# Two neighbouring blocks in one transfer, two products of one weight in one matmul, and a new order of work

## The chip, the cores and the metric

The kernel runs on one core of a Trainium2 chip. Its time is the device time of one execution in microseconds. The core's engines run beside each other and are tied by semaphores: TensorE (PE, with PEld for its weight loads), VectorE (DVE), ScalarE (ACT), GpSimd (POOL), and SyncE (SP), which here only issues transfers (DMAs). 16 DMA engines move the bytes between the chip's main memory and the on-chip SBUF. PE writes its products to PSUM, which has eight banks of 512 fp32 columns.

## What is computed

An attention over the channels (normalised along N) is followed by a soft mixture of experts, all in fp32, with B = 4, N = 5056, C = 256, 8 experts of 4 slots each:

```python
qn = q / (norm(q, axis=1) + 1e-06);  kn = k / (norm(k, axis=1) + 1e-06)
a = softmax(kn.transpose(0, 2, 1) @ qn / tau)          # [B, C, C]
x = (v @ a).reshape(B * N, C)
logits = x @ phi                                       # [B*N, 32]
slot_input = softmax(logits, axis=0).T @ x             # 32 slots, 4 to an expert
slot_out = relu(slot_input @ w1[e]) @ w2[e]            # for each expert e
out = softmax(logits, axis=1) @ slot_out               # [B*N, C]
```

## The kernel before

Everything large is moved in blocks of 1 MiB: 128 partitions with a row of 8 KB each. There are 40 blocks of q and k together (`raw0` to `raw39`, ten to a batch), 20 of v, 10 of v transposed on the host (`x4` to `x13`; for the other v blocks PE transposes, L492), 8 of w1, 8 of w2, and 20 MiB of output. In main memory each 8 KB row of an input is followed by 512 bytes of padding; the output has none. SBUF holds 23 slots of one block. The table `SLOTS` gives each block its slot, and a block may be loaded when the last reader of the slot's former block is done. Since all transfers are issued by SP, one after another, a load that waits for its slot holds up every load behind it. At most eight transfers are under way: each has one of eight semaphores and waits for that one's former transfer.

What happens to one q/k block `u` (four tiles of 128 rows): `square` (ACT, L301 and L303) writes the squares, `add` (DVE, L321) sums them for the column norms. A part of the tiles (`NS[u]`, two to four of four from `u` = 1 on, 117 tiles in all) is split into a rounded high part and a low rest: `cast` (ACT, L288) writes the high part, `low` (POOL, L292) subtracts it. `score` (L345) then multiplies on PE: for a split tile and each half `m` of the key's columns three products of 256 columns (high key with high query, high key with low query, low key with high query), for a tile that is not split one product in plain fp32. All of them add into the same 256 columns of `S`, and the two halves `m` lie in one PSUM bank. At the end of a batch `att_evict` (ACT, L368) copies `S` to SBUF, and `att_cols` to `att_m` (L373 to L457) make the softmax and from it the matrix `M` that turns v into logits.

For a v block: `logits` (PE, L507 and L512), copies and maxima (ACT L535, DVE L539, L545), and, in groups of three and two blocks, exponents and `gather` (PE, L612). After the last group come the experts: `up` (PE, L762, needs w1), `down` (PE, L795, needs w2), and then the output: `out_mul` (PE, L830 and L845), `out_evict` (ACT and DVE in turn, L862) and `store` (SP, L866 to L872). The weights w2 come in two halves, `w2_0_*` for output columns 0 to 127 and `w2_1_*` for the rest; outputs named `oh` need only one half. The last loads are those of `w2_1_*`.

The order of all of it is written out: the steps are put in a list `plan`, and the table `ORDER` says in which order they are recorded. `BANKS` gives each PSUM tile its bank. `wake` (L255) multiplies ones with ones: eight such products stand ahead of the first score.

Of the kernel before, what the change touches and what calls it, by code (L numbers as in the profile page):

```python
# [8 lines left out]
F32 = mybir.dt.float32  # L9
# [15 lines left out]
NT = [3 if u % (2 * UB) == 2 * UB - 1 else 4 for u in range(NU)]  # L25
# [4 lines left out]

SAME = set()
# [6 lines left out]
WAKES = ((-8, 8),)  # L38


ORDER = [
# [60 lines left out]
]  # L102
SLOTS = {
# [64 lines left out]
}  # L168


def run(plan):
    for x in ORDER:
# [927 lines left out]
```

## Time and profile before

| | us |
|---|---|
| time, median of 3 runs | 271.57 (271.47 to 271.7) |
| span of the profiled execution | 269.6 |
| what lies around the span, against the median | 2.0 |
| PE, POOL, ACT, DVE busy in the span | 244.9, 169.6, 207.1, 201.0 |
| transfers of SP's queue, as a share of 16 engines' span | 98.8% |

How to read it: the busy times say how much each engine had to do, not which of them sets the end. For that one looks at what runs without a gap, at what the last work waited for, and at how far ahead of its use each transfer was issued. The profiled execution's own time beside its span was not recorded; the 2.0 us are the difference to the median.

### The profile page before, as it was taken

Reading aid. Unit: us, or ns where it says so; the run is one execution under the profiler, and the core shown is the slowest. Engines: PE = TensorE matmul, PEld = TensorE weight load, DVE = VectorE, ACT = ScalarE, POOL = GpSimd, SP = SyncE. Lnnn points to the kernel's source line nnn. Section 1 sums busy time; section 2 is a strip of 40 time slices with the busy share of each in tenths; the row PEclk is TensorE's granted clock in tenths of the full one; section 3 lists DMA queues with packets and bytes.
Section 4 is the critical chain, followed back from the end, with each engine's and each line's share of the span. In section 5 each row is a group of like instructions: output and inputs, shape, how many; then the busy total and the mean of one; then the engine's idle time right before and its main releaser. Section 6 shows DMA issues by size and latency. Waiting matters only on the chain.

```text
span 269.6 us, 6368 instructions
## 1 busy us (share of the span) xinstructions
PE 244.9 (91%) x2490; PEld 205.4 (76%) x2490; DVE 201.0 (75%) x406; ACT 207.1 (77%) x331; POOL 169.6 (63%) x135
## 2 busy tenths in 40 slices
PE   6999999999999999999999999999999889989300
PEld 6799899999998987879879968985647677666200
DVE  1388688978799989889998788897785747795400
ACT  3999899999999999999999987586826536566200
POOL 1399989999999998989999999731206030000000
PEclk9999999999999999999999999999999999999555
DMA  7999999999999999999999999999999999999995
GB/s 272 428 424 419 417 419 420 423 418 416 424 414 419 422 417 422 423 414 416 421 421 418 420 427 413 420 420 422 413 423 422 412 418 395 420 424 422 424 425 227
DMA packets 15725, 110.80 MB, mean 411 GB/s; under 512 B 1872, under 2 KB 1872, under 8 KB 3024
## 3 DMA queue, kind: packets, MB, share of 16 engines
q1 hardware_dynamic: 15696, 110.40, 98.8%
q8 instruction: 19, 0.31, 0.5%
q14 instruction: 10, 0.08, 0.1%
HBM read 89.43 MB, written 20.97 MB: 409 GB/s over the span
## 4 chain that ended last, share of the span: by engine, by line
PE 78%; DMA 11%; DVE 2%; ACT 1%; issue 1%; SPq 0%; ACTq 0%
PE S L345 42%; PE L L512 7%; PE G L612 7%; PE T L492 6%; DMA w<-in_moe_w_dram 6%; PE op_None L845 4%; DMA out_dram<-o 3%; PE op L830 3%; DMA raw<-in_qk_dram 3%; PE H L762 2%; PE O L795 1%; PE Mp L445 1%; ACT o L862 1%; PE S L354 1%; PE nn L373 1%; PE aTp L433 1%
## 5 line engine op out<-in xcount | busy, mean ns | idle before, releaser
L292 POOL TENSOR_TENSOR hl<-raw,hl 128x512 fp32r<-128x512 f32 x117 | 146.5, 1291 | 14.3 <-ACT hl L288 14.3
L321 DVE TENSOR_TENSOR A<-sq,A 128x512 f32<-128x512 f32 (+1 forms) x144 | 94.5, 690 | 20.6 <-ACT sq L303 18.5
L345 PE MATMUL S<-hl 128*128 128x256 f32 x702 | 100.0, 292 | 0.0
L345 PEld LDWEIGHTS S<-hl 128*128 128x128 f32 x702 | 89.1, 190 | 3.5 <-issue 2.3
L303 ACT ACTIVATE sq<-raw 128x2048 f32<-128x2048 f32 (+2 forms) x40 | 71.6, 1806 | 0.2 <-DMA raw<-in_qk_dram 0.2
L288 ACT CAST hl<-raw 128x1024 fp32r<-128x1024 f32 (+1 forms) x69 | 61.0, 916 | 2.9 <-DMA raw<-in_qk_dram 1.4
L345 PE MATMUL S<-raw 128*128 128x256 f32 x156 | 38.3, 381 | 1.7 <-DMA raw<-in_qk_dram 1.7
L345 PEld LDWEIGHTS S<-raw 128*128 128x128 f32 x156 | 27.7, 190 | 5.2 <-DMA raw<-in_qk_dram 2.5
L492 PE MATMUL T<-ident,v 128*128 128x128 f32 x156 | 21.8, 274 | 0.5 <-DVE maxs L539 0.5
L710 POOL TENSOR_TENSOR nat<-nat,cm 128x1280 f32<-128x1280 f32 x4 | 9.4, 2352 | 19.0 <-DVE cm L707 19.0
L725 POOL TENSOR_TENSOR nat<-nat,cs 128x1280 f32<-128x1280 f32 x4 | 9.4, 2348 | 16.9 <-DVE cs L722 16.9
L862 ACT COPY o<-op_None 128x512 f32<-128x512 f32 x22 | 12.0, 592 | 10.2 <-PE op_None L845 9.0
L512 PE MATMUL L<-x,M 128*32 128x256 f32 (+1 forms) x320 | 19.3, 379 | 0.0
L492 PEld LDWEIGHTS T<-ident,v 128*128 128x128 f32 x156 | 17.8, 141 | 1.8 <-DVE maxs L539 0.7
L612 PE MATMUL G<-v,dn 128*32 128x256 f32 x312 | 18.7, 380 | 0.0
L830 PE MATMUL op<-cT,so 32*128 32x256 f32 x144 | 17.5, 417 | 0.7 <-ACT so L817 0.4
L862 DVE COPY oh<-op 128x256 f32<-128x256 f32 x36 | 12.9, 411 | 5.3 <-PE op L830 5.0
L862 DVE COPY o<-op_None 128x512 f32<-128x512 f32 x22 | 13.9, 680 | 2.7 <-PE op_None L845 2.6
L830 PEld LDWEIGHTS op<-cT,so 32*128 32x128 f32 x144 | 12.3, 183 | 4.3 <-ACT o L862 1.5
L612 PEld LDWEIGHTS G<-v,dn 128*32 128x32 f32 x312 | 10.7, 110 | 6.3 <-issue 0.5
L512 PEld LDWEIGHTS L<-x,M 128*32 128x32 f32 x320 | 10.3, 110 | 5.7 <-issue 0.7
L862 ACT COPY oh<-op 128x256 f32<-128x256 f32 x36 | 11.9, 384 | 2.7 <-PE op L830 2.7
(122 smaller groups left out, 279.8 us busy)
## 6 DMA issues: line engine op xcount, KB each, us to landing
raw<-in_qk_dram SPq DMA_DIRECT2D x38, 1024.0 KB, 13.6
v<-in_v_dram SPq DMA_DIRECT2D x16, 1024.0 KB, 13.8
w<-in_moe_w_dram SPq DMA_DIRECT2D x16, 1024.0 KB, 19.8
out_dram<-o SPq DMA_DIRECT2D x11, 1024.0 KB, 10.2
x<-in_vt_dram SPq DMA_DIRECT2D x10, 1024.0 KB, 13.5
out_dram<-oh SPq DMA_DIRECT2D x8, 1024.0 KB, 8.8
v<-in_v_dram SPq DMA_DIRECT2D x4, 896.0 KB, 13.8
raw<-in_qk_dram SPq DMA_DIRECT2D x2, 768.0 KB, 11.5
```

The source lines that it names most:

```text
L288: act.copy(parts(u, lo, hi)[:, :, 0::2, :], raws[u][:, lo:hi])
L292: pool.tensor_tensor(hl[:, :, 1::2, :], raws[u][:, lo:hi], hl[:, :, 0::2, :].bitcast(F32), op=ALU.subtract)
L303: act.activation(sqs[u][:, n : NT[u]], raws[u][:, n : NT[u]], AF.Square)
L321: dve.tensor_tensor(a[r], s[r, j], a[r], op=ALU.add)
L345: pe.matmul(S_[:, m], l, r, start=first, stop=False, skip_group_check=True)
L492: pe.transpose(tp[:, P * jj : P * jj + P], vtile(p, 4 * h + jj)[:, P * m : P * m + P], ident)
L512: pe.matmul(L[S * g : S * g + S, :n, :], M[:, m, :], x[:, :n, S * g : S * g + S], start=m == 0 and g not in void, stop=m == 1, skip_group_ ...
L612: pe.matmul(gp[S * g : S * g + S, :C], dn[:, x, j, :], vtile(p, j), start=x == 0 and j < G, stop=x == n - 1 and j >= G,)
L710: pool.tensor_tensor(nat[b], nat[b], st[b]["cm"].broadcast_to([P, 8 * PB, S]), op=ALU.subtract)
L830: pe.matmul(ops[b, p, hf, g], so[r, hf], cT[b][r, 8 * p : 8 * p + 8, :].rearrange("s j t -> s (j t)"), start=True, stop=True,)
L845: pe.matmul(ops[b, p, hf, g][:, h, :], cT[b][r, 4 * i : 4 * i + 4, :].rearrange("s j t -> s (j t)"), rhs[r], start=True, stop=True,)
L862: (dve.tensor_copy if g % 2 else act.copy)(dst, ops[b, p, hf, g])
```

## The change

- **Transfers.** The 86 input blocks are put by the host into two arrays in main memory, `one` (rows of 8 KB) and `two` (two blocks side by side, rows of 16 KB; both with the same 512 bytes behind each row). The list `GROUPS` names 8 blocks that come alone and 39 pairs. A pair needs two neighbouring slots that are free at the same time, and both blocks land together. The list `OUTS` does the same for the output: 17 stores, four of them pairs of 2 MiB. The output array now has rows of 16 KB, without padding; blocks that are stored alone fill half of such a row. All bytes are the same.
- **Slots.** 9 slots are tiles as before (numbers 0 to 8), 14 are neighbours in one tile, `arena`. `SLOTS` is new.
- **Score.** The two products that have the high key as weight become one of 512 columns; the two halves of the columns are added later. So `S` takes two banks a batch, one for each `m`. `att_evict` adds the halves, on DVE instead of ACT.
- **Wake.** Ten products of ones ahead of the first score instead of eight; one more that stood near the end moves to the start too, and one of three goes to the stretch of the stores.
- **Order.** `ORDER`, `SLOTS` and `BANKS` are new throughout.

```diff
-WAKES = ((-8, 8),)
+WAKES = ((-8, 10),)
+NT_SLOTS, NA_SLOTS = 9, 14
+GROUPS = [
+    ("q0",), ("q1",), ("q2",), ("q3",), ("v4",), ("v9",), ("v14",), ("v19",), ("w1_4", "w1_5"),
...
+    arena = const.tile([P, NA_SLOTS, W], F32, name="arena")
...
+    def load(g):
+        n = sum(cols(x) for x in GROUPS[g])
+        src = (one, two)[len(GROUPS[g]) - 1][PLACE[g]]
+        sp.dma_start(run_of(GROUPS[g])[:, :n], src[:, :n])
...
     def score(u, j):
...
-                parts_ = [(hl[:, w, cols], hl[:, y, :]) for w, y in ((2, 0), (2, 1), (3, 0))]
-            for l, r in parts_:
-                pe.matmul(S_[:, m], l, r, start=first, stop=False, skip_group_check=True)
...
+            mul(m, hl[:, 2, cols], hl[:, 0:2, :].rearrange("p y c -> p (y c)"), 0, 2 * C)
+            mul(m, hl[:, 3, cols], hl[:, 0, :], 0, C)
...
     def att_evict(b, m):
-        act.copy(st[b]["ssb"][:, m], st[b]["S"][:, m])
+        both = st[b]["S"][m].rearrange("p (y c) -> p c y", y=2)
+        dve.tensor_reduce(mine(b, "ssb", [P, 2, C], "ssb")[:, m], both, axis=AX.X, op=ALU.add)
...
+    def store(g):
+        n = W // 2 if OUTS[g][0] in HALF else W * len(OUTS[g])
+        k, x = OPLACE[g]
+        sp.dma_start(oa[k][:, x * W : x * W + n], run_of(OUTS[g])[:, :n])
```

What stands on the queues now, in three places. **SP in the middle of the loads.** `raw` are q/k blocks, `x` transposed v blocks; `PE_49`, `DVE_49` and the like are the engines that a load waits for, `DMAHW` the transfers. Before:

```order
L266 DMA raw_946<-in_qk_dram 128x2048 [waits PE_49,DMAHW4_49,Activation_49,Pool_49]
L266 DMA raw_978<-in_qk_dram 128x2048 [waits DMAHW5_49,Activation_49]
L266 DMA raw_996<-in_qk_dram 128x2048 [waits DMAHW6_49,Pool_49]
L266 DMA raw_1014<-in_qk_dram 128x2048 [waits DMAHW7_49,PE_49]
L487 DMA x_1017<-in_vt_dram 128x2048 [waits DMAHW0_49,DVE_49]
L266 DMA raw_1082<-in_qk_dram 128x2048 [waits DMAHW1_49,PE_49,Pool_49]
```

And in the change, where these are the pairs `x4,x5`, `q32,q33`, `x6,x7`, `q30,q31`, then `v4` alone, then `x8,x9` and `v5,v6`:

```order
L260 DMA arena<-in_two_dram 128x4096 [waits DMAHW0_49,DMAHW5_49,Activation_49,Pool_49]
L260 DMA arena<-in_two_dram 128x4096 [waits DMAHW6_49,PE_49]
L260 DMA arena<-in_two_dram 128x4096 [waits DMAHW3_49,PE_49,DMAHW7_49,Activation_49,Pool_49]
L260 DMA arena<-in_two_dram 128x4096 [waits DVE_49,PE_49,DMAHW2_49,Activation_49,Pool_49]
L260 DMA arena<-in_one_dram 128x1792 [waits DMAHW5_49,DMAHW1_49,PE_49]
L260 DMA arena<-in_two_dram 128x4096 [waits Activation_49,Pool_49]
L260 DMA arena<-in_two_dram 128x4096 [waits PE_49,DMAHW4_49,Activation_49,Pool_49]
```

A load of the change waits for the readers of two former blocks, and carries twice the bytes.

**SP at the end, the stores.** Names: `oh` and `o` are output blocks. Before:

```order
L869 DMA out_dram<-oh_1_1_3125 128x2048
L866 DMA out_dram<-o_3_3184 128x2048
L866 DMA out_dram<-o_2_3221 128x2048
L866 DMA out_dram<-o_4_3241 128x2048
L866 DMA out_dram<-o_0_3218 128x2048
```

In the change:

```order
L260 DMA arena<-in_two_dram 128x4096 x13
L903 DMA out_dram<-arena 128x1024
L903 DMA out_dram<-arena 128x2048 x5
L903 DMA out_dram<-arena 128x4096
L903 DMA out_dram<-arena 128x2048
L903 DMA out_dram<-arena 128x4096
```

The last thirteen loads are all pairs; of the stores only four are, and a store of half a block now comes first.

**PE, the first blocks.** `hl` is a split pair of tiles, `raw` (`q` in the change) a block that is used as it came. Before:

```order
L345 MATMUL S_139<-raw_144 128x256 x4
L345 MATMUL S_139<-raw_131 128x256 x4
L345 MATMUL S_139<-hl_146 128x256 x6
L345 MATMUL S_139<-raw_163 128x256 x4
L345 MATMUL S_139<-hl_146 128x256 x6
```

In the change:

```order
L400 MATMUL S_0_138<-q_144 128x256
L400 MATMUL S_1_139<-q_144 128x256
L400 MATMUL S_0_138<-hl_160 128x512
L400 MATMUL S_0_138<-hl_160 128x256
L400 MATMUL S_1_139<-hl_160 128x512
L400 MATMUL S_1_139<-hl_160 128x256
```

Six products of 256 columns for a split tile became two of 512 and two of 256.

## Rows read from the trace of the kernel before

**Rows 1.** The page: span, and in 40 slices the DMA engines' busy tenths.

```profile
span 269.6 us, 6368 instructions
DMA  7999999999999999999999999999999999999995
GB/s 272 428 424 419 417 419 420 423 418 416 424 414 419 422 417 422 423 414 416 421 421 418 420 427 413 420 420 422 413 423 422 412 418 395 420 424 422 424 425 227
```

**Rows 2.** The page, part 3: transfers by queue; q1 is SP's.

```profile
DMA packets 15725, 110.80 MB, mean 411 GB/s; under 512 B 1872, under 2 KB 1872, under 8 KB 3024
q1 hardware_dynamic: 15696, 110.40, 98.8%
q8 instruction: 19, 0.31, 0.5%
HBM read 89.43 MB, written 20.97 MB: 409 GB/s over the span
```

**Rows 3.** The chain that ended last: start us, us, what.

```profile
8.19 24.27 PE S L345 x146
...
84.77 0.71 PE S L345 x6
...
197.64 5.31 PE H L762 x48
202.95 15.05 DMA w<-in_moe_w_dram
...
218.14 3.73 PE O L795 x128
```

**Rows 4.** Transfer issues: engine, count, KB each, median us from issue to landing.

```profile
raw<-in_qk_dram SPq DMA_DIRECT2D x38, 1024.0 KB, 13.6
w<-in_moe_w_dram SPq DMA_DIRECT2D x16, 1024.0 KB, 19.8
out_dram<-o SPq DMA_DIRECT2D x11, 1024.0 KB, 10.2
```

**Rows 5.** Timeline of the start: start us, us, what [idle before <-releaser].

```profile
0.74 7.75 SPq L266 DMA_DIRECT2D raw<-in_qk_dram  x10
1.05 3.41 PE L255 MATMUL wake<-ones 128*128 128x128 f32 x16 [1.05 <-DVE ones L241]
5.70 1.99 PE L345 MATMUL S<-raw 128*128 128x256 f32 x8 [1.23 <-DMA raw<-in_qk_dram]
8.19 1.13 PE L345 MATMUL S<-raw 128*128 128x256 f32 x4 [0.49 <-DMA raw<-in_qk_dram]
```

**Rows 6.** Transfers from 27 to 29 us: packets, MB, share of 16 engines.

```profile
DMA packets 254, 0.80 MB, mean 402 GB/s; under 512 B 160, under 2 KB 160, under 8 KB 160
q1 hardware_dynamic: 254, 0.80, 101.9%
```

**Rows 7.** The same from 30 to 100 us.

```profile
DMA packets 4170, 29.39 MB, mean 420 GB/s; under 512 B 459, under 2 KB 459, under 8 KB 715
q1 hardware_dynamic: 4162, 29.29, 100.9%
```

**Rows 8.** Stretches: us, busy of PE, PEld, DVE, ACT, POOL, clock, DMA share, GB/s.

```profile
90.00:120.00 30.00, 30.00 (x327) 25.62 (x330) 26.86 (x54) 29.64 (x47) 27.29 (x23) 1.00 1.01 419
232.00:250.00 18.00, 16.57 (x152) 11.63 (x155) 13.20 (x27) 10.15 (x22) 0.00 (x0) 0.99 1.01 421
```

**Rows 9.** SP's waits, 30 to 160 us: us, times, longest.

```profile
SPq L266 <- PE S L345: 28.5, 9, 5.3
SPq L266 <- DVE A L321: 16.7, 6, 5.4
SPq L468 <- POOL hl L292: 7.6, 4, 4.5
```

**Rows 10.** Groups by form: count | busy us, mean ns | idle before.

```profile
L292 POOL TENSOR_TENSOR hl<-raw,hl 128x512 fp32r<-128x512 f32 x117 | 146.5, 1291 | 14.3 <-ACT hl L288 14.3
L368 ACT COPY ssb<-S 128x256 f32<-128x256 f32 x8 | 2.9, 372 | 1.0 <-PE S L345 1.0
L378 DVE TENSOR_REDUCE rn<-nn 128x4 f32<-128x512 f32 x4 | 2.7, 676 | 0.7 <-PE nn L373 0.7
L707 DVE TENSOR_REDUCE cm<-nat 128x40 f32<-128x1280 f32 x4 | 5.9, 1468 | 0.0
```

More of the change, by code (lines that the diff above doesn't have):

```diff
@@ L23 @@
 GR = (3, 2)
-NT = [3 if u % (2 * UB) == 2 * UB - 1 else 4 for u in range(NU)]
+NQ = [3 if u % (2 * UB) == 2 * UB - 1 else 4 for u in range(NU)]
 NS = [0, 2, 2, 2, 2, 2, 2, 2, 2, 2, 3, 3, 3, 3, 3, 3, 3, 3, 3, 3, 3, 3, 3, 3, 3, 3, 3, 3, 3, 3, 4, 4, 4, 4, 4, 4, 4, 4, 4, 3]
@@ L180, in colnorm_attention_soft_moe @@
     tc: tile.TileContext,
-    qk: bass.AP,
-    v8: bass.AP,
-    vt8: bass.AP,
+    one: bass.AP,
+    two: bass.AP,
     vhalf: bass.AP,
     few: bass.AP,
-    w1: bass.AP,
-    w2: bass.AP,
     oa: bass.AP,
@@ L200, in colnorm_attention_soft_moe, with block, run_of @@
     ps = ctx.enter_context(tc.tile_pool(name="ps", bufs=1, space=PSUM, reuse_waits="tile"))
-    def slot(name, shape, dt=F32):
-        return large.tile(shape, dt, tag=f"s{SLOTS[name]}", name=name)
+    arena = const.tile([P, NA_SLOTS, W], F32, name="arena")
+    blocks = {}
+    def block(name):
+        if name not in blocks:
+            k = SLOTS[name]
+            if k < NT_SLOTS:
+                blocks[name] = large.tile([P, W], F32, tag=f"s{k}", name=name)
+            else:
+                blocks[name] = arena[:, k - NT_SLOTS]
+        return blocks[name]
+    def run_of(names):
+        if len(names) == 1:
+            return block(names[0])
+        k = SLOTS[names[0]] - NT_SLOTS
+        assert SLOTS[names[1]] == k + 1 + NT_SLOTS
+        for x in names:
+            block(x)
+        return arena[:, k : k + 2].rearrange("p k w -> p (k w)")
+    def load(g):
+        n = sum(cols(x) for x in GROUPS[g])
+        src = (one, two)[len(GROUPS[g]) - 1][PLACE[g]]
+        sp.dma_start(run_of(GROUPS[g])[:, :n], src[:, :n])
     def short(name):
-        t = slot(name, [P, 2 * C, 4]).rearrange("p c x -> p (c x)")
-        return t[:, : 8 * PB * S].rearrange("p (j s) -> p j s", s=S)
+        return block(name)[:, : 8 * PB * S].rearrange("p (j s) -> p j s", s=S)
     def bank(name):
@@ L237, in colnorm_attention_soft_moe, with mine @@
     now = {}
+    def mine(b, key, shape, tag):
+        if key not in st[b]:
+            st[b][key] = bpool.tile(shape, F32, tag=tag, name=f"{key}{b}")
+        return st[b][key]
     def constants():
@@ L255, in wake, with raw, sq @@
             pe.matmul(w[:, :P], ones, ones, start=True, stop=True)
-    raws, sqs, hls = {}, {}, {}
-    def load_qk(u, lo, hi):
-        b, i = divmod(u, UB)
-        if u not in raws:
-            raws[u] = slot(f"raw{u}", [P, 4, 2, C])
-        src = qk[b, i][:, : 8 * C].rearrange("p (j x c) -> p j x c", x=2, c=C)
-        sp.dma_start(raws[u][:, lo:hi], src[:, lo:hi])
+    hls = {}
+    def raw(u):
+        return block(f"q{u}").rearrange("p (j x c) -> p j x c", x=2, c=C)
+    def sq(u):
+        return block(f"sq{u}").rearrange("p (j x c) -> p j x c", x=2, c=C)
     split = {}
@@ L325, in join, with sums, mul @@
         dve.tensor_tensor(a, st[b]["odd"], a, op=ALU.add)
-    def sums(b):
+    begun = set()
+    def sums(b, m):
         if "S" not in st[b]:
-            st[b]["S"] = bank(f"S{b}").rearrange("p (m c) -> p m c", m=2)
-            return st[b]["S"], True
-        return st[b]["S"], False
+            st[b]["S"] = [bank(f"S{b}_{x}") for x in range(2)]
+        first = (b, m) not in begun
+        begun.add((b, m))
+        return st[b]["S"][m], first
     def score(u, j):
         b, i = divmod(u, UB)
-        S_, first = sums(b)
+        def mul(m, l, r, lo, hi):
+            S_, first = sums(b, m)
+            pe.matmul(S_[:, lo:hi], l, r, start=first, stop=False, skip_group_check=True)
         for m in range(2):
@@ L338, in score @@
             if j >= NS[u]:
-                parts_ = [(raws[u][:, j, 1, cols], raws[u][:, j, 0, :])]
-            else:
-                k, x = split[u, j]
-                hl = hls[k][:, x]
-                parts_ = [(hl[:, w, cols], hl[:, y, :]) for w, y in ((2, 0), (2, 1), (3, 0))]
-            for l, r in parts_:
-                pe.matmul(S_[:, m], l, r, start=first, stop=False, skip_group_check=True)
-                first = False
+                mul(m, raw(u)[:, j, 1, cols], raw(u)[:, j, 0, :], 0, C)
+                continue
+            k, x = split[u, j]
+            hl = hls[k][:, x]
+            mul(m, hl[:, 2, cols], hl[:, 0:2, :].rearrange("p y c -> p (y c)"), 0, 2 * C)
+            mul(m, hl[:, 3, cols], hl[:, 0, :], 0, C)
     def score_halves(u):
         b = u // UB
-        raw = raws[u][:, 3]
-        both = [(sums(b), slice(0, HD)), (sums(b + 1), slice(HD, P))]
+        rw = raw(u)[:, 3]
         for m in range(2):
-            for (S_, first), r in both:
+            for x, r in enumerate((slice(0, HD), slice(HD, P))):
+                S_, first = sums(b + x, m)
                 pe.matmul(
-                    S_[:, m],
-                    raw[r, 1, P * m : P * m + P],
-                    raw[r, 0, :],
-                    start=first and m == 0,
+                    S_[:, :C],
+                    rw[r, 1, P * m : P * m + P],
+                    rw[r, 0, :],
+                    start=first,
                     stop=False,
@@ L429, in att_turn @@
     def att_turn(b, m):
-        if m == 0:
+        if "tp" not in st[b]:
             st[b]["tp"] = bank(f"aTp{b}").rearrange("p (n c) -> p n c", n=2)
@@ L477, in vtile @@
         b, q = divmod(p, PB)
-        return vh[:, b // 2] if q == PB - 1 and j == 7 else vs[p][:, j]
+        return vh[:, b // 2] if q == PB - 1 and j == 7 else block(f"v{p}").rearrange("p (j c) -> p j c", c=C)[:, j]
     def xt(p):
-        if p not in xs:
-            xs[p] = slot(f"x{p}", [P, 2, 8 * P])
-        return xs[p]
-    def load_vt(p):
-        b, q = divmod(p, PB)
-        sp.dma_start(xt(p), vt8[b, q][:, : 16 * P].rearrange("p (m t) -> p m t", m=2))
+        return block(f"x{p}").rearrange("p (m t) -> p m t", m=2)
     def turn(p, h, m):
@@ L576, in exps @@
     def exps(b, gi, c, n):
-        if c == 0:
+        if (b, gi) not in zs_:
             st[b]["z", gi] = bpool.tile([P, 3], F32, tag=f"z{gi}", name=f"z{b}_{gi}")
@@ L772, in relu @@
         if r not in hss:
-            hss[r] = slot(f"hs{r}", [P, 2 * F])[:, :F]
+            hss[r] = block(f"hs{r}")[:, :F]
         act.activation(hss[r][:, x * UT : x * UT + UT], hps[r, x], AF.Relu, scale=rz[:, r : r + 1])
@@ L784, in back_h @@
         if r not in hTs:
-            hTs[r] = slot(f"hT{r}", [P, 2 * NF, P])[:, :NF]
+            hTs[r] = block(f"hT{r}").rearrange("p (f c) -> p f c", c=P)[:, :NF]
         (act.copy if x else dve.tensor_copy)(hTs[r][:, 4 * x : 4 * x + 4, :], htp[r, x])
@@ L902, in colnorm_attention_soft_moe @@
         for x, j in enumerate(js):
-            at(u + (0.55 if late else 0.4) + 0.1 * x, add, u, j)
+            at(u + 0.4 + 0.1 * x, add, u, j)
         if i == UB - 1:
@@ L906, in colnorm_attention_soft_moe @@
         halves = i == UB - 1 and b % 2 == 0
-        js = [j for j in range(NT[u]) if j >= NS[u] and not (halves and j == 3)] + list(range(NS[u]))
+        js = [j for j in range(NQ[u]) if j >= NS[u] and not (halves and j == 3)] + list(range(NS[u]))
         for x, j in enumerate(js):
@@ L986, in colnorm_attention_soft_moe @@
     at(3.6, load_vh)
-    for e in range(8):
-        at(42.2 + 0.01 * e, load_w1, e)
-    for h in range(2):
-        for k in range(4):
-            at(T0 - 1 + 0.3 * k + h, load_w2, h, k)
+    for g in range(len(GROUPS)):
+        at(-5, load, g)
     for b in range(B):
@@ L1024, in colnorm_attention_soft_moe @@
                 at(t + 0.1, out_evict, b, p, None, g)
-            at(t + 0.2, store, b, p, None)
+            OAT[f"o{b}_{p}"] = t + 0.2
             t += 0.5
+    for g, names in enumerate(OUTS):
+        at(max(OAT[x] for x in names), store, g)
     run(plan)
@@ L1055 @@
     x = x.reshape(B, UB, 4, P, 2 * C).transpose(0, 1, 3, 2, 4)
-    add("qk", apart(x.reshape(B, UB, P, 8 * C)))
+    data = {f"q{u}": x.reshape(NU, P, 8 * C)[u] for u in range(NU)}
     x = np.zeros((B, PB * 8, P, C), np.float32)
@@ L1061 @@
     x = x.reshape(B, PB, 8, P, C)
-    add("v8", apart(x.transpose(0, 1, 3, 2, 4).reshape(B, PB, P, 8 * C)))
-    x = x.reshape(B, PB, 8 * P, 2, P).transpose(0, 1, 4, 3, 2)
-    add("vt8", apart(x.reshape(B, PB, P, 16 * P)))
+    y = x.reshape(B, PB, 8 * P, 2, P).transpose(0, 1, 4, 3, 2).reshape(NP, P, W)
+    x = x.transpose(0, 1, 3, 2, 4).reshape(NP, P, W)
+    for p in range(NP):
+        data[f"v{p}"], data[f"x{p}"] = x[p], y[p]
+    w1, w2 = (np.asarray(inputs[x]) for x in ("moe_w1", "moe_w2"))
+    x = w2.reshape(4, 2, P, 8, 2, P).transpose(4, 0, 2, 1, 3, 5).reshape(8, P, W)
+    for e in range(8):
+        data[f"w1_{e}"], data[f"w2_{e // 4}_{e % 4}"] = w1[e].reshape(P, W), x[e]
+    for k, name in enumerate(("one", "two")):
+        if not NLOAD[k]:
+            args.append(None)
+            continue
+        a = np.zeros((NLOAD[k], P, (k + 1) * W), np.float32)
+        for g, x in zip(GROUPS, PLACE):
+            if len(g) == k + 1:
+                a[x] = np.concatenate([data[y] for y in g], axis=1)
+        add(name, apart(a))
     add("vh", v[:, nf:].reshape(2, P, C).transpose(1, 0, 2))
@@ L1073 @@
     add("few", np.concatenate([phi, sel.reshape(P, 2), tau], axis=1))
-    w1, w2 = (np.asarray(inputs[x]) for x in ("moe_w1", "moe_w2"))
-    add("moe_w1", apart(w1.reshape(8, P, -1)))
-    x = w2.reshape(4, 2, P, 8, 2, P).transpose(4, 0, 2, 1, 3, 5)
-    add("moe_w2", apart(x.reshape(2, 4, P, -1)))
-    out_ap = nc.dram_tensor("out_0_dram", (B * PB, P, 8 * C), F32, kind="ExternalOutput").ap()
+    out_ap = nc.dram_tensor("out_0_dram", (NOUT, P, 2 * W), F32, kind="ExternalOutput").ap()
     args.append(out_ap)
```

140 lines of the change are left out of this document (61 added, 79 removed), and 249 rows, old and new, of tables (BANKS, GROUPS, ORDER, SLOTS).

## The prediction

> **What bounds the kernel now.** I read the slices first [rows 1]. The DMA engines stand at 9 tenths in 38 of 40 slices, and the bytes move at 412 to 428 GB/s in all whole slices but one of 395. SP's queue alone is busy for 98.8% of 16 engines' span [rows 2]. So the transfers run from the first load to the last store. Next comes the chain [rows 3]. It names PE for most of the span, from 8.19 us on and without a gap for long, and that could pass for the bound. But its end tells the order of things: the experts' first product is through at 202.95, then PE waits 15.05 us for w2, and only at 218.14 does the work go on that makes the second half of the output. PE was 15 us early at the one place where it meets the last load, and the stores behind that run at 421 GB/s [rows 8]. **The time is the transfers' time**: 110.40 MB at the pace of the DMA engines, provided that SP issues early enough. It does: from issue to landing the median q/k load takes 13.6 us [rows 4], while the very first, with nothing ahead of it, is issued at 0.74 and used at 5.70, 4.96 us later; the next is used at 8.19, so a transfer takes 2.49 us [rows 5]. The difference, 13.6 - 4.96 = 8.6 us, is the **cover**: so much later could a median load be issued before the engines ran dry.
>
> **The rows of 16 KB.** The bytes stay, the packets fall. One transfer of 1 MiB is 128 rows and, as the count shows, 16 small packets: 107 transfers of 128 rows, 2 x 128 for the two small inputs and 109 x 16 give 13,696 + 256 + 1,744 = 15,696, the row's number [rows 2]. Two transfers are 288 packets, a pair 144. What does a packet cost beside its bytes? Two stretches answer, since one of them holds many small packets. From 27 to 29 us 254 packets with 402 GB/s x 2 us = 0.804 MB took 101.9% of 16 x 2 us = 32.6 us of engine time [rows 6]; from 30 to 100 us 4,162 packets with 29.29 MB took 100.9% of 1,120 = 1,130.1 us [rows 7]. The first scaled to the second's bytes (x 36.4) is 9,253 packets in 1,187.6 us: 5,091 packets more, 57.5 us more, 11 ns each. The short stretch is cut at its ends by part of a packet, so that the figure may lie between 9 and 14 ns; and a long row may yet be slower by itself or be cut up again, so its floor is zero. I take 10 ns, near the measured value and on its lower side because packets overlap by about 1%. A pair then saves 144 x 10 / 16 = 0.09 us on each engine. 39 pairs of loads give 3.5 us, 4 of stores 0.4 us; **together -3.9 us** (0 to -5.4 at 14 ns), all on the path, as the queue has no gaps.
>
> The rows thus show 11 ns a packet. The Trainium skill (DMA: Bandwidth & Descriptors, section Why small descriptors are slow) names a fixed overhead of about 3 cycles a packet; with the same page's 850 MHz that is 3.5 ns, and by it the sum of this part would be an estimated 1.4 us instead of 3.9. [...]
>
> **Pairs and their slots.** This is the term that can give it back. A pair waits for the later of two slots, and SP holds everything behind it. A q/k block with three split tiles is through on POOL in 3 x 1.29 = 3.9 us [rows 10], so of two blocks that are worked on in turn the second leaves 3.9 us after the first. And both land together, so the first is there 2.49 us later than alone. Cover of 8.6 - 3.9 - 2.5 = 2.2 us is left for a median load, and the faster transfers use some 1.5 to 2 us of it by 150 us. That is close to nothing. Against it stands that only the worst delay counts and not their sum (once the queue is late, the next load is measured against the late queue), and that PE, for which SP waits longest [rows 9], gets lighter. The nearest rows for a gap are SP's longest waits of 4.5 to 5.4 us, all covered today. I take **+0.8 us** of idle queue, between 0 and 4; the value lies near the low end because the pairs can be made of blocks that leave together.
>
> **The score.** Six products of a split tile take 0.71 us [rows 3]. Their columns stay 1,536; only a product and a weight load in three go. So PE gains between 0 and, if the joined product costs no more than one of 256 columns, 0.24 us a tile, 0 to 28 us over 117 tiles; I take some 5 us, as the columns have to pass. On the path this is **0**: PE is 15 us early at w2 already, and an earlier PE waits there longer. It does add cover through the slots.
>
> **The sum of the halves.** Eight copies of 0.37 us leave ACT, eight reductions of 512 columns come to DVE: the reduction L378 of 512 columns from PSUM takes 0.68, the one of 1,280 columns 1.47 [rows 10], so 0.68 to 1.47 each, and I take 0.7, 5.6 us in all. In the fullest stretch DVE is busy for 26.86 of 30 us, ACT for 29.64 [rows 8], so the load moves to the engine with more room. What queues behind are the sums of squares, which release slots. A batch's chain to `M` gets 0.3 us longer for each half; the v blocks behind it are covered: **0**, and 0.6 us a batch on the cover if not.
>
> **Wake and start.** Eight products take 3.41 us and end before the first block's use at 5.70 [rows 5]; eleven take 4.7 and end at 5.8. PE starts 0.1 us later with nothing lost, since the transfers don't wait for it: **0**. The first four loads stay single, so the first block lands as before.
>
> **The stores.** Half of the output needs only `w2_0`; its 4.5 MiB, 11 us of transfers, lie between the last load and the first store of the second half, which takes 3.73 us of PE [rows 3] and then evictions. So the queue stays fed: **0**, and 1 us if a 2 MiB store waits for its second block.
>
> **Sum.** -3.9 + 0.8 = -3.1 us: a span of 266.5 after 269.6, and with the same 2.0 us around it a median of **268.5 us** after 271.57.
>
> **The rivals.**
> - *The pairs take most of it back.* Idle queue of 2 to 3.3 us, not 0.8: 269.6 to 271.0. For it speaks the 2.2 us that are left of the cover; against it the lighter PE. Chance 0.15.
> - *The rows are no gain.* If a row of 16 KB is moved as two of 8 KB, a pair saves only its 16 small packets, 0.01 us, 0.4 us in all: 271.2, no change that can be measured. Rows of 8 KB are the longest on SP's queue, so no row excludes it. Chance 0.09.
> - *Slower: slots run out.* Place: the pairs `x4,x5` to `v5,v6`, about 90 to 120 us, where PE, ACT and POOL are all busy for 27 to 30 of 30 us [rows 8] and every load waits for two or three of them. Price: each us by which the later slot is late beyond the cover, at the worst load. It decides from 3.9 us of idle queue on, that is if the second slot of a pair leaves 8.6 + 3.9 - 2.5 = 10 us after the first, two and a half blocks of POOL's work. 5 to 7 us idle give 272.7 to 274.7. Chance 0.13.
> - *Slower: the stores.* Their rows now lie 16 KB apart in main memory without padding, 8 KB before. If that halved their rate, 20.97 MB at 421 GB/s would take 50 us more: 318. Stores with rows 8 KB apart show no harm [rows 8]. Chance 0.02. The Trainium skill (DMA: Bandwidth & Descriptors, Latency and other measured facts) has such a rule for row pitches of 512 KiB and more; no run here shows it.
> - *More.* 13 ns a packet and no gap at all: -5 us, 266.5. Chance 0.09.
>
> **How the numbers follow.** The forecast, 267.1 to 269.6, has 0.52. The range from 266.7 to 271.3 takes in the first two rivals and part of the last and leaves out some 0.2. A difference of 0.2% (0.54 us) is about what a measurement of this kernel can tell from none. Faster: 0.52 + 0.15 + 0.09 = 0.76; same: 0.09; slower: 0.15.
>
> **What would show it.** In the profile of the change SP's queue must have 47 + 17 + 2 = 66 transfers, 64 x 128 + 256 + 66 x 16 = 9,504 packets with 110.40 MB; the rows are cut up if there are more. The slices in the loads' stretch should stand at some 427 GB/s instead of 420 (2 MiB in 4.89 us instead of 4.98). A gap in the queue would show as a slice clearly below its neighbours between 85 and 160 us, with SP waiting for POOL or ACT. PE should still wait for w2 near the end, by about 15 us and more. The prediction is wrong if the rate in the full slices has not risen, or if PE no longer waits for w2: then another engine sets the end.

## The result, and the profile after

| | before | after |
|---|---|---|
| time, median | 271.5 us (271.46 to 271.7, 6 runs) | 273.35 us (272.2 to 274.75, 6 runs) |
| ratio to before | | 1.0064 (1.0043 to 1.0086) |
| profiled execution: time, span | not recorded, 269.6 | 272.2, 270.4 |

The change makes the kernel 0.64% slower; 268.5 us were forecast, and the range ended at 271.3. The profiled execution of the kernel after is its fastest run, 1.15 us below the median. Its runs lie 2.5 us apart, those of the kernel before 0.24.

The page after, span, slices and transfers, beside [rows 1, 2]:

```profile
span 270.4 us, 5786 instructions
DMA  7999999999999999999999999999999999999995
GB/s 273 428 439 431 417 427 432 425 394 408 383 417 427 419 397 397 426 427 427 420 424 420 426 431 435 425 422 424 419 429 423 411 410 393 420 379 407 418 427 229
...
q1 hardware_dynamic: 9504, 110.40, 97.7%
```

The packets are 9,504, as counted ahead: the long rows are moved as long rows. The fastest slices stand at 425 to 439 GB/s where 412 to 428 stood. But slices 9 to 11 (394, 408, 383), 15 and 16 (397, 397) and 34 to 37 (393, 420, 379, 407) are low. Transfers came late there: by the times of landing in the trace, four pairs between 63 and 106 us landed 5.4 to 6.1 us after the load before them instead of 4.9. Part 6, beside [rows 4] (count, KB each, median us from issue to landing):

```profile
arena<-in_two_dram SPq DMA_DIRECT2D x37, 2048.0 KB, 11.1
out_dram<-arena SPq DMA_DIRECT2D x10, 1024.0 KB, 7.3
```

A load of twice the bytes is there 11.1 us after its issue, not 13.6. Less was queued ahead of it. The chain, beside [rows 3] (start us, us, what):

```profile
3.30 20.80 DMA arena<-in_two_dram
24.14 13.33 PE S L400 x68
...
197.27 8.38 PE H L802 x64
...
219.97 1.88 PE O L835 x64
```

No step of it waits 15 us for `w2` any more. Stretches, beside [rows 8] (us, busy of PE, PEld, DVE, ACT, POOL, clock, DMA share, GB/s):

```profile
60.00:90.00 30.00, 30.00 (x237) 25.22 (x238) 27.94 (x49) 29.83 (x41) 30.00 (x25) 1.00 1.00 413
90.00:120.00 30.00, 29.75 (x255) 23.11 (x247) 26.74 (x50) 29.89 (x43) 29.55 (x24) 1.00 1.00 409
232.00:250.00 18.00, 17.11 (x165) 13.70 (x159) 13.46 (x27) 11.27 (x27) 0.00 (x0) 1.00 0.96 398
```

Against a full 427 GB/s the first two lost 30 x (14 + 18) / 427 = 2.2 us of transfer time, the last 18 x 29 / 427 = 1.2 us. The DMA share of the first two stays at 1.00 all the same: a late packet counts as busy while it lasts, and some of 16 KB lasted 0.9 to 2.2 us there, where the median is 0.61. So the share alone doesn't show the loss. SP's waits from 30 to 160 us, beside [rows 9] (us, times, longest):

```profile
SPq L260 <- PE S L400: 31.7, 4, 23.0
SPq L260 <- POOL hl L352: 25.1, 7, 6.2
SPq L260 <- DVE A L380: 24.2, 6, 6.2
```

No single engine is late: SP waits for PE, POOL and DVE in turn, for up to 23.0, 6.2 and 6.2 us at a time. The groups by form, beside [rows 10]:

```profile
L352 POOL TENSOR_TENSOR hl<-arena,hl 128x512 fp32r<-128x512 f32 x111 | 139.2, 1295 | 4.8 <-ACT hl L348 4.6
L400 PE MATMUL S<-hl 128*128 128x512 f32 x234 | 92.1, 427 | 0.1
L400 PE MATMUL S<-hl 128*128 128x256 f32 x234 | 65.5, 280 | 0.0
L431 DVE TENSOR_REDUCE ssb<-S 128x256 f32<-128x512 f32 x8 | 5.5, 682 | 0.0
```

A sum of two halves on DVE takes 0.68 us. The joined product takes 427 ns and its neighbour 280, so a half of a split tile takes 0.71 us; before, three products of 292 ns took 0.88. The products overlap, though: on the page the busy time of all products of split tiles is 98.6 us, and before, by the same view, 100.0. PE's whole busy time went from 244.9 to 243.9 us.

In both traces the last load lands at 218.0 us. So the loads gained nothing in the end, and the stores after them took 51.4 us instead of 50.3.

### The profile page after: what moved, and what is told of

It reads as the page before. It is cut to its first block, busy times and chain, and to the rows that moved or that the text cites. A ratio compares the mean times of both kernels' runs of the same rounds, so it can differ in the third digit from the quotient of the medians.

```text
span 270.4 us, 5786 instructions
## 1 busy us (share of the span) xinstructions
PE 243.9 (90%) x2260; PEld 193.3 (71%) x2260; DVE 207.9 (77%) x414; ACT 205.1 (76%) x323; POOL 169.9 (63%) x135
## 3 DMA queue, kind: packets, MB, share of 16 engines
q1 hardware_dynamic: 9504, 110.40, 97.7%
## 4 chain that ended last, share of the span: by engine, by line
PE 69%; DMA 8%; ACT 7%; DVE 6%; issue 2%; SPq 1%; DVEq 0%
PE S L400 31%; DMA arena<-in_two_dram 8%; PE T L538 6%; PE op L870 5%; PE op_None L885 5%; PE L L558 5%; PE G L658 5%; PE H L802 3%; PE O L835 3%; DVE A L380 3%; ACT sq L362 2%; ACT hl L348 1%; PE Mp L503 1%; ACT arena L362 1%; ACT a L474 1%
## 5 line engine op out<-in xcount | busy, mean ns | idle before, releaser
L352 POOL TENSOR_TENSOR hl<-arena,hl 128x512 fp32r<-128x512 f32 x111 | 139.2, 1295 | 4.8 <-ACT hl L348 4.6
L400 PE MATMUL S<-hl 128*128 128x512 f32 x468 | 98.6, 354 | 0.1
L380 DVE TENSOR_TENSOR A<-sq,A 128x512 f32<-128x512 f32 (+1 forms) x82 | 54.8, 690 | 19.2 <-ACT sq L362 17.6
L348 ACT CAST hl<-arena 128x1024 fp32r<-128x1024 f32 (+1 forms) x66 | 57.8, 907 | 1.6 <-DMA arena<-in_two_dram 1.3
L380 DVE TENSOR_TENSOR A<-arena,A 128x512 f32<-128x512 f32 (+1 forms) x62 | 41.5, 691 | 2.2 <-ACT arena L362 0.8
L362 ACT ACTIVATE sq<-arena 128x2048 f32<-128x2048 f32 (+2 forms) x19 | 34.5, 1819 | 0.0
L362 ACT ACTIVATE arena<-arena 128x2048 f32<-128x2048 f32 (+1 forms) x17 | 30.7, 1810 | 0.0
L400 PE MATMUL S<-arena 128*128 128x256 f32 x116 | 29.0, 382 | 1.1 <-DMA arena<-in_two_dram 1.1
L400 PEld LDWEIGHTS S<-arena 128*128 128x128 f32 x116 | 20.3, 189 | 5.0 <-DMA arena<-in_two_dram 1.6
L538 PE MATMUL T<-ident,arena 128*128 128x128 f32 x142 | 19.9, 274 | 0.1
## 6 DMA issues: line engine op xcount, KB each, us to landing
arena<-in_two_dram SPq DMA_DIRECT2D x37, 2048.0 KB, 11.1
```

The lines of the kernel that those rows point to most:

```text
L348: act.copy(parts(u, lo, hi)[:, :, 0::2, :], raw(u)[:, lo:hi])
L352: pool.tensor_tensor(hl[:, :, 1::2, :], raw(u)[:, lo:hi], hl[:, :, 0::2, :].bitcast(F32), op=ALU.subtract)
L362: act.activation(sq(u)[:, n : NQ[u]], raw(u)[:, n : NQ[u]], AF.Square)
L380: dve.tensor_tensor(a[r], s[r, j], a[r], op=ALU.add)
L400: pe.matmul(S_[:, lo:hi], l, r, start=first, stop=False, skip_group_check=True)
L538: pe.transpose(tp[:, P * jj : P * jj + P], vtile(p, 4 * h + jj)[:, P * m : P * m + P], ident)
```

## The experiments

All ratios are to the kernel before, run on the same chip, with 95% intervals. The changed kernel stands at 1.0064 (1.0043 to 1.0086).

### Which part of the change costs

Loads in single transfers:

```diff
-        sp.dma_start(run_of(GROUPS[g])[:, :n], src[:, :n])
+        for y, name in enumerate(GROUPS[g]):
+            sp.dma_start(block(name)[:, : cols(name)], src[:, y * W : y * W + cols(name)])
```

> Each pair of loads goes as two transfers of 1 MiB, each of which waits for its own slot alone; order, slots, score and stores stay those of the changed kernel. Theory A (a pair holds the queue up, since it waits for the later of two slots and both blocks land together): the idle time among the loads (about 3 us in the changed kernel) goes, the pace falls back from 4.89 to 4.97 us for two blocks (39 x 0.08 = 3 us), so the loads still end at about 218 us and the time is 272.3 to 273.5, with a spread under 0.5 us between runs. Theory B (the new order of the compute work lets go of the slots late, pairs or not): the idle time stays, the pace is lost as well, loads end at 220 to 221.5 us, time 275 to 276.5.

Measured: 274.5 us, 1.0111 (1.0086 to 1.0137). The last load lands at 219.3 us. Neither theory is met in full: some gaps go (416 GB/s from 60 to 120 us, where full speed of single loads is 420), but the pace is lost, and together it is slower. By the medians the pairs are worth about 1.2 us in this order of work (the two intervals meet at 1.0086); **they are not what costs.**

Stores in single transfers, the same edit in `store`:

> The four pairs of stores go as two transfers each; all else as in the changed kernel. Theory T (a store of 2 MiB waits for its second block and the queue runs dry, 1.2 us at the blocks o2_2 and o2_3): 272.0 to 272.5 us. Rival (the stores only hand on what is late on PE and the evictions): within 0.3 us of the changed kernel, 273.0 to 273.7.

Measured: 273.41 us, 1.0066 (1.0047 to 1.0085). No difference: the pairs of stores are innocent.

The joined product taken apart, the sum of halves a copy on ACT again:

```diff
-            mul(m, hl[:, 2, cols], hl[:, 0:2, :].rearrange("p y c -> p (y c)"), 0, 2 * C)
+            mul(m, hl[:, 2, cols], hl[:, 0, :], 0, C)
+            mul(m, hl[:, 2, cols], hl[:, 1, :], 0, C)
...
-        dve.tensor_reduce(mine(b, "ssb", [P, 2, C], "ssb")[:, m], both, axis=AX.X, op=ALU.add)
+        act.copy(mine(b, "ssb", [P, 2, C], "ssb")[:, m], st[b]["S"][m][:, :C])
```

> The joined product of 512 columns is taken apart into two of 256 again, all three products add into 256 columns, and ACT copies the sum as before; pairs, slots and order as in the changed kernel. Theory A (pairs): nothing of this is on the path, 273.0 to 274.0 us. Theory B in the form that the sums on DVE hold up what frees the slots: 271.7 to 272.7. Rival (the joined products make PE lighter, and without them the split tiles are held longer): 274 to 276.

Measured: 274.7 us, 1.0106 (1.0069 to 1.0142). By the medians the joined product is worth 1.3 us, but the intervals overlap. All three edits together:

> All three at once: loads and stores in transfers of 1 MiB, score and sum of halves as before; what stays of the change is the order, the slots and the wake. Theory A (pairs are the cause): 271.3 to 272.0 us, loads end at 218 us and the queue is idle for under 1 us. Theory B (order and slots are the cause): 274.5 us or more, loads end after 220 us.

Measured: 274.05 us, 1.0088 (1.0056 to 1.012). **What is left of the change here is the order, the slots and the wake, and that alone is 2.5 us slower than the kernel before.** The new arrays in main memory are left as well, but they don't slow the transfers (421 GB/s from 30 to 60 us in the next section's kernel with single transfers). None of the three visible parts costs anything that these runs can tell; the tables that came with them do.

### The transfers by themselves

The changed kernel's transfers in their order, nothing computed; then the same with single transfers:

```diff
-        f(*a)
+        if f.__name__ in ("load", "store", "load_few", "load_vh"):
+            f(*a)
```

> Only the changed kernel's transfers, in its order, with nothing computed: 8 single loads and 39 pairs, 13 single stores and 4 pairs (the stores send whatever lies in two slots). No load waits for an engine, so this is the pace by itself. Theory A (rows of 16 KB are faster by what the count of packets gives): two blocks in 4.88 to 4.90 us, and some 3 to 3.9 us less than the same transfers as singles, about 263 us. Rival (in a queue that never runs dry the long rows bring nothing): the same time as the singles within 0.5 us.

> The same transfers alone, each pair as two of 1 MiB with rows of 8 KB. Theory A: 2.48 us a block, about 266 us, 3 to 3.9 us above the pairs. Rival: within 0.5 us of the pairs. Either way the distance of the kernel before (271.57) to this time is what it loses beside the transfers.

Measured: 264.28 us (ratio 0.9731, 0.9717 to 0.9746) and 267.66 (0.9856, 0.9841 to 0.9871). The page of the pairs, span and queue (packets, MB, share of 16 engines):

```profile
span 262.5 us, 125 instructions
...
q1 hardware_dynamic: 9504, 110.40, 99.3%
```

The same of the singles:

```profile
span 265.5 us, 158 instructions
...
q1 hardware_dynamic: 15696, 110.40, 99.9%
```

The long rows save 3.38 us in 43 pairs, 0.079 us each; over 144 packets on 16 engines that is 8.7 ns a packet. The pace was read rightly. But the kernel before takes 3.9 us more than the same bytes in single transfers (in the new order and arrays; its own order wasn't run alone), the kernel after 9.1 us more than its own transfers.

### Which engine lets go of the slots late

Three kernels each took work off one engine. On PE:

```diff
-            mul(m, hl[:, 3, cols], hl[:, 0, :], 0, C)
+            if m == 0:
+                mul(m, hl[:, 3, cols], hl[:, 0, :], 0, C)
```

> The changed kernel, but of the products with the low key as weight only the first half of the columns is made: 117 products of 256 columns fewer, some 33 us less on PE out of 244. Pairs, slots and orders stay. Theory H (the new order keeps the split tiles until a PE that reads them late, and so takes the slots from the loads): the idle time among the loads falls from about 3 us to under 1, the loads end near 215.5, and the time comes to 270.5 or below. Rival (the sums of squares on DVE, or the pairs' own double wait, hold the slots): idle time and time stay, 272.5 to 274.

On DVE:

```diff
-            dve.tensor_tensor(a[r], s[r, j], a[r], op=ALU.add)
+            dve.tensor_tensor(a[r, :C], s[r, j, :C], a[r, :C], op=ALU.add)
```

> The changed kernel, but the sums of squares on DVE take 256 of the 512 columns: some 0.27 us less for each of 140 additions, 38 us of DVE's 208. Pairs, slots and orders stay. Theory D (squares are held until a DVE that adds late): the idle time among the loads falls below 1 us, time 271 or below. Theory H (PE is what is late): the squares leave sooner, yet the split tiles do not, and the time stays within 0.7 us of 273.35.

And, on PE again, no reader at all for a stretch:

```diff
+            if 18 <= u < 28:
+                continue
             k, x = split[u, j]
```

> The changed kernel, but PE leaves out the products of the split tiles of the blocks 18 to 27 (28 tiles, some 20 us of PE between 60 and 118 us); the tiles are still made by ACT and POOL, and nobody reads them afterwards. Theory H (split tiles wait for their place in PE's order and so keep slots): their slots come free some 6 us earlier, the idle time among the loads between 60 and 125 us falls from 3 us to under 1, loads end at 216 us or before, time 271.9 or below. Rival (what POOL and ACT take is what sets the slots free, not the place in PE's order): idle time and time stay, 272.7 to 274.

Measured: 273.72 us (1.0068, 1.004 to 1.0096), 273.42 (1.0057, 1.0034 to 1.008) and 273.89 (1.0087, 1.0074 to 1.01); from 60 to 120 us the transfers ran at 413, 409 and 409 GB/s. (The blocks 18 to 27 have 30 such tiles, not 28.) My theories H and D both fall. The traces do show that the new order keeps a pair of split tiles longer, 13.7 us from its first write to the end of its last product against 8.9 (means of the 35 and 33 pairs begun between 60 and 150 us). But taking away the readers of such tiles, or some of PE's work, or almost a fifth of DVE's, brings neither the gaps nor the time down. The first kernel took less off PE than I had reckoned: the 117 products of 280 ns overlap with others, and PE's busy time fell by 7.1 us (243.9 to 236.8), not by 33.

### The old order with pairs

Each engine works through its old order, while the blocks are dealt out anew to nine tiles and fourteen neighbouring slots; first with single loads, then with 24 pairs:

```diff
-PAIRS = []
+PAIRS = [('raw8', 'raw3'), ('raw6', 'raw14'), ('raw7', 'raw9'), ('raw12', 'raw10'), ('raw13', 'raw16'),
```

> The kernel before: every engine works through its old order, score and stores are the old ones, and all loads are single, in the old sequence. Only the places are new: nine tiles and fourteen neighbouring slots, dealt out anew to the same blocks. It is the ground for the next kernel. All theories: 271.2 to 272.0 us, loads end at 218 us.

> The same, with 24 of the loads joined in pairs with rows of 16 KB (chosen where two neighbouring slots came free in the old times with some 5 us of cover left). Theory O (the pairs are sound and the new order of work is what costs): 24 x 0.08 = 1.9 us less than the one with singles, 269.2 to 270.1, loads end at 216 us. Rival (a pair drains the queue under any order): the gain is given back, 271 us or more.

Measured: 272.08 us (1.0024, 1.0015 to 1.0033) and 271.8 (1.0015, 1.0002 to 1.0027). The new places by themselves cost some 0.6 us. Here the pairs do what they should to the loads: the last one lands at 216.6 us instead of 218.1. And yet only 0.3 us of the forecast 1.9 arrive. This is the run that shows where the gain goes. PE from 213 us on in the kernel with pairs (start us, us, what):

```profile
213.02 6.11 PE L772 MATMUL op<-cT,so 32*128 32x256 f32 x64 [0.36 <-ACT so L759]
219.06 0.30 PE L737 MATMUL O<-w,hT 128*32 128x128 f32 x2
```

and its stretch around the last loads, columns as above:

```profile
203.00:218.00 15.00, 14.22 (x234) 10.22 (x228) 10.06 (x22) 8.24 (x20) 4.65 (x2) 1.00 0.88 369
```

The last weights are there at 216.6, as the trace has it, and PE comes to them at 219.06, without having waited: it was busy with the first half of the output. The transfers have nothing to carry in the meantime and fall to 369 GB/s. The same place in the kernel before, PE's timeline:

```profile
206.53 3.70 PE L795 MATMUL O<-w,hT 128*32 128x128 f32 x128
210.65 0.49 PE L811 MATMUL fo<-ob,fold 128*128 128x128 f32 x2 [0.41 <-DVE ob L807]
211.49 6.11 PE L830 MATMUL op<-cT,so 32*128 32x256 f32 x64 [0.35 <-ACT so L817]
218.14 1.08 PE L795 MATMUL O<-w,hT 128*32 128x128 f32 x32 [0.54 <-DMA w<-in_moe_w_dram]
```

And its stretch:

```profile
203.00:218.00 15.00, 13.82 (x226) 10.38 (x218) 10.08 (x25) 9.71 (x24) 4.65 (x2) 1.00 1.01 417
```

In the 15 us in which [rows 3] let PE wait for `w2`, PE was busy for 13.8 us. It waited for the last load 0.54 us, not 15.

### The engines by themselves

If PE and its neighbours were on time by half a microsecond only, the kernel should hardly get faster without any loads to wait for. A load into a neighbouring slot that was filled once carries 64 columns (changed kernel; the old order likewise):

```diff
+        if slots <= seen:
+            for y, name in enumerate(names):
+                sp.dma_start(block(name)[:, :64], src[:, y * W : y * W + 64])
+            return
+        seen.update(slots)
         sp.dma_start(run_of(names)[:, :n], src[:, :n])
```

> What the engines take by themselves, old order: the kernel with the old order on new places and single loads, but a load into a neighbouring slot that was filled once before carries only 64 columns (32 KB), so that from about 60 us on hardly anything has to be moved; stores stay whole. The data are then those of earlier blocks. Theory E (the engines' own line is as long as the transfers' line, and the two were balanced): the experts' first product still starts at 193 to 197 us, and the time is 266 to 271. Theory D (transfers bind, as the prediction had it): the engines run ahead, the experts start before 185 us, the time is below 258.

> The same for the changed kernel: pairs, slots, score and order are its own, but loads into slots filled once before carry 64 columns a block. Theory E: the experts' first product starts at 193 to 197 us as in the changed kernel itself (197.2), the time is 268 to 272, so that faster transfers cannot show. Theory D: the experts start before 185 us, the time is below 258.

Measured: 270.09 us (0.9949, 0.9922 to 0.9975) with the old order, 271.2 (0.9978, 0.9952 to 1.0004) with the new one. The experts' first product starts at 198.02 and 196.92 us in the two traces, so the engines don't run ahead. The page of the new one, 40 slices:

```profile
PE   8998999999999999999999999999999898999200
...
ACT  3799999999999999999999944677635536674300
POOL 1668999999999999999999996054044400000000
...
DMA  7999992226000000101022000101000199999995
```

From the seventh slice to the thirty-second the transfers stand at 0 to 2 tenths, with one slice of 6, and the time is within 1% of what it was. Its stretch from 60 to 120 us:

```profile
60.00:120.00 60.00, 59.98 (x487) 48.59 (x486) 54.91 (x100) 59.84 (x82) 59.73 (x49) 1.00 0.14 45
```

That of the old order:

```profile
60.00:120.00 60.00, 59.93 (x549) 54.40 (x551) 53.12 (x99) 59.62 (x85) 57.43 (x47) 1.00 0.39 134
```

PE, ACT and POOL have under 0.5 us of 60 to spare in the new order, with next to nothing to load. The old order is the weaker test, since its nine tiles are still loaded in full: 39.3 of 89.4 MB are read there, 22.3 in the new one. But from 60 to 200 us its PE is hardly ever idle:

```profile
60.00:200.00 140.00, 139.93 (x1495) 118.76 (x1497) 123.41 (x252) 125.33 (x213) 115.42 (x89) 1.00 0.40 138
```

And it waits for a load once in the whole execution (us, times, longest):

```profile
PE S L294 <- DMA raw<-in_qk_dram: 0.8, 1, 0.8
```

It comes to the second half of the experts' last product at 217.99 us, with the last load there since 199.0; in the kernel before it came there at 218.14. **The engines have a line of work as long as the transfers' line, and it is this one that the change doesn't shorten.** (The first 41 us of loads, some later ones and all stores are still in these times, so 270 us aren't the engines' work alone; the stores fill the last 50 us of them.) Which engine sets it:

```diff
+            if m == 0:
+                mul(m, hl[:, 3, cols], hl[:, 0, :], 0, C)
...
+        k = 1 if 1 <= i <= 7 else 2
+        act.activation(sq(u)[:, n : NQ[u], :k], raw(u)[:, n : NQ[u], :k], AF.Square)
```

> The changed kernel with the short reloads, and of the products with the low key as weight only the first half of the columns (some 33 us less on PE). If PE's line sets the engines' time, it falls by 15 us or more against the kernel with the short reloads alone; if ACT and POOL set it, by less than 4.

> The changed kernel with the short reloads, and in 28 of the 40 blocks only half of the columns is squared on ACT and added on DVE (some 27 us less on ACT, 30 on DVE); PE and POOL as before. If ACT or DVE set the engines' time, it falls by 8 us or more against the kernel with the short reloads alone; if PE or POOL set it, by less than 4.

> The changed kernel with the short reloads, and both reliefs at once: half of the products with the low key left out on PE, half of the columns of 28 blocks neither squared on ACT nor added on DVE. Only POOL keeps its whole work. If POOL's line by itself is as long as the others', the time falls by less than 4 us against the kernel with the short reloads alone (271.2), as each relief by itself did; if PE and ACT only took turns in setting it, by 8 us or more.

Measured: 269.42 us with less on PE (0.9929, 0.991 to 0.9948), 270.1 with less on ACT and DVE (0.993, 0.9902 to 0.9957), 268.34 with both (0.9905, 0.9876 to 0.9934). Against 271.2 that is 1.8, 1.1 and 2.9 us; the second interval overlaps with that of the short reloads alone, the third lies clear of it. The relief on PE was smaller than forecast: its busy time fell from 247.0 to 238.3 us, since the products overlap, so the 15 us or more of the first expectation could not come. ACT lost 20.8 us of busy time, DVE 28.9. From 60 to 120 us in the kernel with both reliefs:

```profile
60.00:120.00 60.00, 57.59 (x482) 43.97 (x485) 45.17 (x102) 53.02 (x82) 60.00 (x50) 1.00 0.12 37
```

PE and ACT have room now, POOL has none: 60.00 of 60. With only one relief the others still filled the stretch (ACT 59.84 and POOL 59.67 with less on PE; PE and POOL 60.00 each with less on ACT and DVE). Its subtractions, 117 times 1.29 us, are 151 us in a row, and the softmaxes, the experts and the output come after them. That POOL is the last line is read from this row; a kernel with less on POOL was not run.

### Two smaller questions

> The changed kernel, but the products and copies of the output blocks that need only the first half of the columns stand ahead of the second half of the experts' last product again, as in the kernel before; with the new order 2.5 MiB of stores were issued when the last load landed at 218 us, with the old one 4. Theory T2 (the stores run dry for 1 to 2 us since the evictions come late): 272.2 to 272.8. Rival (the gaps come from the later blocks, where PE and the copies set the pace): 273.0 to 273.7.

Measured: 276.25 us, 1.0169 (1.0148 to 1.019). The moved steps also change part of the output, so this isn't quite the same work, and the transfers fall to 368 GB/s from 218 to 250 us. It settles nothing.

> The changed kernel, but three of the products of ones that it moved to the stretch of the stores stand ahead of the experts again, where the kernel before had them. Theory W (without them PE's clock falls as the experts begin, 0.66 of the full clock from 195 to 200 us against 1.00 before, and the experts' first product takes 8.45 us): the clock stays up there and the time falls by 0.5 to 1.2 us, to 272.2 to 272.9. Rival (the clock falls with them as well, as it did in the kernel with the old order and new places, or the loss is hidden): 273.0 to 273.7.

Measured: 273.68 us, 1.0079 (1.0053 to 1.0104), no difference that can be told. In its trace the clock does stay at 1.00 from 195 to 200 us, so the fall of the clock at this place isn't what makes the changed kernel slower by the medians. That the clock plays no part elsewhere isn't shown by it.

## Why the prediction was wrong, by its steps

**What bounds the kernel: the step that failed.** I read "PE was 15 us early" from the chain's entry of 15.05 us for `w2` [rows 3]. A chain names the one path back from the end; that it runs along a transfer for 15 us doesn't say that PE stood still. In that time PE ended the experts' first product (at 204.64, not 202.95), made the first half of the second one and the output that needs only it, and came to the last load 0.54 us ahead of it. The signs were in the rows: PE at 30.00 of 30 us and ACT at 29.64 [rows 8] in a stretch that I took to be set by transfers. The kernel before is balanced: 267.7 us for its bytes in single transfers alone (in the new order), about 270.1 for the engines with less than half of the loads (old order on new places), 271.5 for both. Shortening one of two such lines by 3 us can't bring 3. With the new order's engines at 271.2, and none of their ten runs below 269.4, the forecast of 268.5 was out of reach whatever the transfers did.

**The rows of 16 KB.** Right in kind: -3.4 us measured by the transfers alone against -3.9, since a packet takes 8.7 ns and not 10. The 3 cycles a packet that the Trainium skill names (DMA: Bandwidth & Descriptors, section Why small descriptors are slow), worked out in the prediction to an estimated 1.4 us for all pairs, are too few by these runs.

**Pairs and their slots: +0.8 forecast.** About 2.2 us of transfer time went between 60 and 120 us. With the pairs of loads split most of that is gone: 416 GB/s against 420 are 0.6 us. So there the pairs' double wait did cost, some 1.6 us by one trace of each kernel and not 0.8. But the rival "slots run out" had the number (272.7 to 274.7) for a reason that doesn't carry it: splitting the pairs doesn't bring the time back (274.5). I costed the loss for the pairs, with the order as given; but the order and the slots alone cost 2.5 us. For the order I had no term at all.

**The score: 0.** Undoing it costs 1.3 us by the medians, with intervals that overlap. The reason given for 0, an early PE, is wrong: PE is on the path. The gain on PE was 1.0 to 1.4 us of busy time, not 5.

**The sum of the halves: 0.7 us each, 0 on the path.** The duration is right (0.68). The effect by itself wasn't measured.

**Wake: 0.** Holds by the medians: 273.68 with three products put back. That the clock could fall where they had stood was not foreseen.

**The stores: 0.** Pairing them costs nothing (273.41), and rows 16 KB apart in main memory are no harm: with nothing computed, the pairs' kernel stored at 431 GB/s from 215 to 258 us. But the queue does run dry there, 1.2 us from 232 to 250 us, and more in the old order with pairs: the output is made only just in time, and stores can't start earlier because loads end earlier.

**What would show it.** "The prediction is wrong if PE no longer waits for w2: then another engine sets the end" was the right check; it would have failed in the kernel before already, had I looked at PE between 203 and 218 us.

**What stays open.** Where in the new order the 2 us lie that it costs beside the old one (274.05 against 272.08, both with single transfers, the old score and new places). Of these 1.1 us are in the engines' line by the medians (271.2 against 270.1, with intervals that overlap, and the new order has the joined product there). The rest may be what engines and transfers take from each other through the slots; which steps of the order do it wasn't found. The runs of the kernel after scatter by 2.5 us, those of the two kernels with short reloads alone by 3.3 and 3.4. Part of that goes along with PE's mean granted clock over a run. With less on ACT and DVE, the three runs at 0.952 and 0.953 took 269.0 to 269.1 us and the four at 0.946 and 0.947 took 270.1 to 270.9. With the short reloads alone in the new order, the three at 0.952 and 0.953 took 269.4 to 269.9 and the six at 0.941 to 0.948 took 271.1 to 272.7, but one at 0.955 took 271.3. The median clock is 0.9475 there and 0.956 in the old order, so the clock may be behind the 1.1 us too. Whether it makes the runs longer wasn't tested. No version was found that beats the kernel before.

## What to carry to other kernels

A queue at 99% shows one bound, not that it is the only one. Before a gain on it is counted, ask for every engine how long it stood idle ahead of the place where it meets the queue's last transfer, from that engine's own timeline and not from the chain; half a microsecond there is the most that a faster queue can bring at that place. The cheapest test is to take the transfers away, or the computing, and see what time is left.

## What the runs showed of the hardware

- A packet costs 8.7 ns of a DMA engine beside its bytes, by two kernels that only move data (264.28 and 267.66 us, 6,192 packets apart on 16 engines). That puts the whole difference on the packets; the kernels are also 43 transfers apart.
- As the experts begin in the changed kernel, PE's granted clock fell to 0.66 of 2.4 GHz on average from 195 to 200 us, that is to 1.2 GHz for about two thirds of it. Ahead of it PE had waited 0.68 us and then done a few small products, by its timeline:

```profile
194.54 0.63 PE L683 MATMUL gt<-fold,gs 128*128 128x32 f32 x4 [0.68 <-DVE gs L673]
195.10 0.66 PE L721 MATMUL slp<-fold,acc 64*128 64x32 f32 x4
```

  The products that follow (ns shortest/median/longest, first and last start us):

```profile
L802 PE MATMUL H<-arena,slT x64: 592/592/1061, 197.2 to 205.1; 128*32 128x512 f32 x64
```

  The longest took 1,061 ns, the median 592. All of them together took 8.45 us, and 7.07 in the kernel before, where the clock stayed at 1.00. With three products of ones ahead of them the clock stayed up as well, and the median time was no shorter (273.68 us).
